# Second layer of a fused attention, MoE and feed-forward kernel: weights requested earlier, into raw buffers alone

## The chip, the cores and the metric

The kernel runs on one core of a Trainium2 chip. TensorE (PE, with PEld for its weight loads) multiplies matrices, VectorE (DVE), ScalarE (ACT) and GpSimd (POOL) do elementwise work, and SyncE (SP) issues most of the DMAs. Each engine executes its own list of instructions strictly in the order in which the program wrote them, and waits at an instruction until the semaphores that it names are reached. What counts is the device time of one execution in microseconds (us).

## The reference

Three stages follow each other. The first is a decayed, unnormalised attention over 8 batches, 8 heads, 576 positions and head size 64. The second is a mixture of 8 experts that sends each of the 4608 tokens (512 numbers each) to one expert. The third, the second layer here, is a dense feed-forward, and the change lies in it:

```python
def _moe2_ref(x, w_in, w_out) -> np.ndarray:      # x: 4608 x 512
    h = x @ w_in                                  # w_in: 512 x 2048
    r = np.maximum(h, 0.0)
    g = r * r
    return (g @ w_out).astype(np.float32)         # w_out: 2048 x 512
```

## The kernel before

**Precision.** Every float32 operand of a large product is split into a rounded part (`hi`) and a remainder (`lo`), and each product is three matmuls, hi by hi, hi by lo and lo by hi. `split` (L1012, L1013) makes the parts: ScalarE writes `hi` with a cast, VectorE then writes `lo` with a subtraction. In the second layer the subtractions are put aside in a list, `los`, and written out where `run_los` is called.

**Tiling of the second layer.** It runs in two passes, one for each half of the 2048 inner columns. A pass goes through nine slots of 512 tokens, and a slot through four quads; so there are 72 quads, numbered 0 to 71, 36 in a pass. Pass one ends with slot 8 (quads 32 to 35), and pass two begins with the same slot (quads 36 to 39). `hquad(n)` multiplies the 512 tokens of the slot by 256 columns of `w_in`. It treats both as 2 by 2 blocks and forms seven products of sums of blocks instead of eight products (Strassen's scheme); that is 42 matmuls of 128x256. Products 1 and 3 go to the PSUM tile `px`, 4 and 2 to `py`, 5 to `pz` (named `pr_all` in the trace), and 7 and 6 are added into `px` again after ScalarE has copied it out. ScalarE copies `px`, `py`, `pz` to the tile `mc`, GpSimd combines them in four operations (L1375 to L1380), VectorE adds the last two products (L1383) and squares what is positive (L1384). The result is split into `gh` (L1387, ScalarE) and `gl` (L1388, VectorE). There is one `mc` tile: the copy of the next quad's `px` waits for `gl` of this quad. `zquad(n)` multiplies `gh` and `gl` by `w_out` (24 matmuls of 128x512) and is written one quad late: TensorE's order is hquad(0), hquad(1), zquad(0), hquad(2), zquad(1), and so on.

**Weights.** The weights of a quad (`WQ`, eight of them, four a pass) are seven sums and plain blocks of `w_in`, split into `wqh` and `wql`. `wq_load` requests the four plain blocks from a scratch tensor `cw`, `wq_sums` forms the five sums on GpSimd (L1041), `wq_split` splits blocks 0 to 3 (128x1024) and then 4 to 6 (128x768). The `w_out` weights of two quads (`WO`, four of them, two a pass) are requested by `wo_load` and split by `wo_split` in two halves. The tokens of a slot are fetched by `x_fetch`, summed by `x_sums` and split by `x_split` and `x_plain` in the same way.

**Buffers.** All these tiles share 20 buffers. `bigt` takes the one that has been idle longest, `drop` gives one back, and the first instruction that writes a taken buffer waits for the last that used it. `wq_load` and `wo_load` take three buffers at once (hi, lo and raw), though only raw, and one block of the hi tile of a `WQ`, are written by the DMAs.

**Order.** It is written out by hand. The table `m2` in `OPT` says at which tick of the last expert slot a step of the second layer stands ('wl 0' is `wq_load(0)`, 'ws' the sums, 'wh' the split). Then comes a branch for rarely needed expert slots (L1329), which no execution here takes. After it, three dictionaries hold the steps of each quad: `before` stands ahead of hquad, `gaps` inside it ahead of the cast to `gh`, `tails` behind zquad of the quad before.

Of the kernel before, what the change touches and what calls it, by code (L numbers as in the profile page):

```python
# [51 lines left out]
def layouts(inputs):  # L52
# [18 lines left out]
    wi = np.ascontiguousarray(inputs["moe2_w_in"].reshape(4, P, 4, 512).transpose(2, 1, 0, 3).reshape(4, P, 2048))  # L71
# [49 lines left out]
    pass  # L121


OPT = dict(manual=True, nbig=10,nlate=10,nx=2,b0=2,bl='SG',rl=2,pz=5,ve=lambda m:'GV' if m<3 or m%4==0 else 'GS',vn=(4,4,2),egn=2,nps=2,npo=1,npt=2,npm=4,nwarm=11,ew=(20,25,32,33),es={23:1,24:1,25:1,26:1,28:1,29:1,30:1,31:1},rlag=1,rlagl=1,rlate=35,rperl=30,e5=5,e6=4,ld=4,rper=8,nw=3,biasat=4,keep=(5,0,4,2),nxw=3,scs=2,e3=13,ylag=2,zlag=2,gb=3,zb=4,cf=(0,6,7,12),cf0=(0,8,9,13),hv=10,zend=1,cwm={0:3},cws={i:(1 if i<4 else 2) for i in range(2,14)},cv0=8,scat=lambda i,n: 2,f3=33,f4=34,f5=34,e0=dict(ro=1,esplit={2:4,3:2,4:2},r1=0,r2=2,r3=2,tab=(7,8,8,9),rec=5,raw=(0,0,1,3),g1=7,split={5:2,6:2,7:2,8:3,9:3,10:2,11:2},xn1=11,tr0=6,tr1=4),hh=3,hl=3,ylag2=1,bs1=dict(regs=1,rec=1,raw=(3,4,5,6),g0=3,g1=7,gn0=(2,)*4,gn1=(2,)*4,split={6:1,7:1,8:2,9:2,10:1,11:2,12:2,13:1,14:2,15:2},tr0=10,tr1=13,cv=1),bs=dict(regs=-9,rec=-9,raw=(0,3,6,8),g0=-4,g1=4,gn0=(1,)*8,gn1=(1,)*8,split={5:1,6:1,7:2,8:2,9:2,10:2,11:2,12:2,13:2},tr0=5,tr1=13,cv=0,f0=7,p0=13,m2={1:('wl 0','xf'),4:('ws 0','xs 0'),5:('xh 0',),6:('wh 0 0',),7:('xs 1',),8:('xh 1',),9:('wh 0 1','wl 1','xs 2'),10:('xh 2','xp 1'),11:('xp 4','ws 1'),12:('wh 1 0',),13:('wh 1 1',)}))


def kernel_body(tc, I, out):
# [1272 lines left out]
    def zquad(n):  # L1400
# [73 lines left out]
    at(gaps, 2, run_los)  # L1474
    for i in range(4):
        at(tails, 32 + i, wq_load, 4 + i)
        at(tails, 33 + i, wq_sums, 4 + i)
        at(gaps, 34 + i, wq_splits, 4 + i)
    for i in range(2):
        at(tails, 34 + 2 * i, wo_load, 2 + i)  # L1480
        at(gaps, 35 + 2 * i, wo_splits, 2 + i)
        at(gaps, 35 + 2 * i, run_los)
    for s in range(len(GSEQ) - 1):
        if s == 8:
            continue
        n, x = 4 * s + (s == 0), s + 1
        at(before, n, x_fetch, x)
        at(tails, n, x_meta, x)
        for i in range(3):
            at(tails, n + i, x_sums, x, i)  # L1490
            d = gaps if n + i + 1 < 4 * x else before
            at(d, n + i + 1, x_split, x, i)
            if i < 2:
                at(gaps, n + i + 1, x_plain, x, (1, 4)[i])
            else:
                at(d, n + i + 1, x_done, x)
# [16 lines left out]
    es.close()

# [14 lines left out]
```

## Time and profile before

| | us |
|---|---|
| median of 3 runs | 1417.16 |
| lowest, highest | 1414.82, 1423.12 |
| the profiled execution | 1433.08 |
| its span, first to last instruction | 1431.3 |
| PE busy in it | 1361.8 (95%) |
| DVE, ACT, POOL busy | 876.4, 517.6, 534.4 |

The profiled execution is a run of its own, taken with the profiler on; all durations of single instructions below come from it. Times of instructions count from the start of its span. The second layer begins at about 634 us and lasts to the end, so it is more than half of the time. Idle time of an engine is given in square brackets ahead of the instruction that ended it, with what it waited for.

### The profile page before, as it was taken

What the parts mean: (1) busy time and instruction counts of PE and PEld (TensorE: products, weight loads), DVE (VectorE), ACT (ScalarE), POOL (GpSimd) and SP (SyncE); (2) the same over time, 40 slices, a digit from 0 to 9 for tenths busy, and PEclk for the clock granted to TensorE, in tenths of its full rate; (3) what the DMA queues carried; (4) which work ended last, traced back from release to release, by engine and by line L of the source; (5) the groups of instructions that cost most, each with busy time, mean ns of one, the idle gap of its engine ahead of it and who ended that gap; (6) DMA issues with size and microseconds to landing.
All of it is one profiled execution on the core that took longest, in us unless ns stands there. A gap on an engine that the chain in (4) does not pass through costs nothing.

```text
span 1431.3 us, 24859 instructions
## 1 busy us (share of the span) xinstructions
PE 1361.8 (95%) x9728; PEld 1191.1 (83%) x9728; DVE 876.4 (61%) x1320; ACT 517.6 (36%) x969; POOL 534.4 (37%) x675
## 2 busy tenths in 40 slices
PE   9999868999999999996999999999989999999996
PEld 7877768988887788896889889898878989989895
DVE  6666747877778677745545454554575556565542
ACT  3223324444344443424433333333443333333321
POOL 0123442644444344224322322223843343434432
PEclk9999979999999999998999999999999999999998
DMA  8788765477655766513111111111231221221210
GB/s 296 215 222 247 204 177 170 139 237 238 208 181 187 243 216 208 164 50 118 59 60 59 31 60 48 43 59 58 91 115 62 89 74 46 88 89 60 88 60 30
DMA packets 105755, 182.08 MB, mean 127 GB/s; under 512 B 25372, under 2 KB 52380, under 8 KB 101276
## 3 DMA queue, kind: packets, MB, share of 16 engines
q1 hardware_dynamic: 96924, 160.96, 36.0%
q0 software_dynamic: 8704, 19.45, 4.4%
q8 instruction: 78, 1.28, 0.4%
q14 instruction: 49, 0.40, 0.1%
HBM read 133.58 MB, written 46.77 MB: 126 GB/s over the span
## 4 chain that ended last, share of the span: by engine, by line
PE 48%; issue 2%; DVE 1%; DMA 1%; ACT 1%; POOL 1%; SPq 0%; POOLq 0%; ACTq 0%; DVEq 0%
PE zp L1420 8%; PE zp L1418 8%; PE zp L1417 8%; PE px L1361 4%; PE px L1363 4%; PE px L1362 4%; PE py L1362 2%; PE py L1363 2%; PE py L1361 2%; PE pr_all L1361 1%; PE pr_all L1363 1%; PE pr_all L1362 1%; DMA wor<-cw 1%; DVE gl L1388 0%; DMA zo<-zA 0%
## 5 line engine op out<-in xcount | busy, mean ns | idle before, releaser
L1417 PE MATMUL zp<-woh,gh 128*128 128x512 f32 x576 | 226.7, 394 | 0.0
L1418 PE MATMUL zp<-wol,gh 128*128 128x512 f32 x576 | 226.6, 393 | 0.0
L1375 POOL TENSOR_TENSOR mc<-mc 128x256 f32<-128x256 f32 x72 | 58.1, 808 | 441.7 <-ACT mc L1374 391.9
L1383 DVE TENSOR_TENSOR mc<-px,mc 128x512 f32<-128x512 f32 x72 | 49.8, 692 | 262.3 <-POOL mc L1379 262.3
L548 POOL DMA_INDIRECT xg<-xl,rix x136 | 139.0, 1022 | 132.5 <-DVE rix L541 75.0
L1420 PE MATMUL zp<-woh,gl 128*128 128x512 f32 x576 | 166.6, 395 | 0.0
L1387 ACT CAST gh<-mc 128x1024 fp32r<-128x1024 f32 x72 | 75.6, 1049 | 237.1 <-DVE mc L1384 233.2
L1388 DVE TENSOR_TENSOR gl<-mc,gh 128x1024 fp32r<-128x1024 f32 x72 | 88.8, 1233 | 90.1 <-ACT gh L1387 90.1
L1420 PEld LDWEIGHTS zp<-woh,gl 128*128 128x128 f32 x576 | 108.5, 188 | 25.2
L1417 PEld LDWEIGHTS zp<-woh,gh 128*128 128x128 f32 x576 | 108.9, 189 | 21.8
L1418 PEld LDWEIGHTS zp<-wol,gh 128*128 128x128 f32 x576 | 108.7, 189 | 21.6
L1361 PE MATMUL px<-xq,wqh 128*128 128x256 f32 x432 | 122.3, 283 | 3.1 <-DVEq L1329 3.1
L639 PE MATMUL yp<-hh,whi 128*128 128x512 f32 (+2 forms) x352 | 123.9, 360 | 1.2 <-ACT hh L619 1.1
L639 PE MATMUL yp<-hh,wlo 128*128 128x512 f32 (+2 forms) x352 | 123.6, 359 | 0.0
L1363 PE MATMUL px<-xq,wql 128*128 128x256 f32 x432 | 122.3, 283 | 1.2 <-DVE wql L1013 1.2
L1362 PE MATMUL px<-xq,wqh 128*128 128x256 f32 x432 | 122.7, 284 | 0.0
L520 DVE TENSOR_TENSOR wlo<-raw,whi 128x512 fp32r<-128x512 f32 x160 | 109.9, 727 | 15.7 <-ACT whi L519 15.1
L1371 ACT COPY mc<-px 128x512 f32<-128x512 f32 x72 | 42.3, 587 | 167.2 <-PE px L1363 143.2
L615 PE MATMUL hp<-xlo,whi 128*128 128x512 f32 (+1 forms) x256 | 98.8, 386 | 0.0
L616 PE MATMUL hp<-xhi,wlo 128*128 128x512 f32 (+1 forms) x256 | 98.7, 385 | 0.0
L614 PE MATMUL hp<-xhi,whi 128*128 128x512 f32 (+1 forms) x256 | 98.7, 385 | 0.0
L519 ACT CAST whi<-raw 128x512 fp32r<-128x512 f32 x160 | 91.0, 618 | 16.2 <-DMA raw<-in_w 14.3
(222 smaller groups left out, 3331.8 us busy)
## 6 DMA issues: line engine op xcount, KB each, us to landing
raw<-in_w SPq DMA_DIRECT2D x34, 1024.0 KB
kqv<-in_kqv SPq DMA_DIRECT2D x108, 256.0 KB
yraw<-yT SPq DMA_DIRECT2D x66, 256.0 KB
zA<-zo SPq DMA_DIRECT2D x36, 256.0 KB
zo<-zA SPq DMA_DIRECT2D x36, 256.0 KB
xl<-xr SPq DMA_DIRECT2D x34, 256.0 KB
craw<-in_wi SPq DMA_DIRECT2D x16, 512.0 KB
cw<-cm SPq DMA_DIRECT2D x32, 256.0 KB
```

The lines of the kernel that those rows point to most:

```text
L520: V.tensor_tensor(out=lo[:, j], in0=raws[i][:, j], in1=hi[:, j].bitcast(F32), op=A.subtract)
L548: G.indirect_dma_start(out=g.x[:, a].rearrange("p k j -> p (k j)"), out_offset=None, in_=xl.rearrange("t (b e) -> (t b) e", b=4)[0:4 * P * ...
L614: PE.matmul(hp, w1h[:, kc, cs], xh[:, kc], start=(kc == 0), stop=False)
L615: PE.matmul(hp, w1h[:, kc, cs], xlo[:, kc], start=False, stop=False)
L616: PE.matmul(hp, w1l[:, kc, cs], xh[:, kc], start=False, stop=(kc == 3))
L639: PE.matmul(hf.yp[dd], w2[:, fb, dd * P:(dd + 1) * P], h, start=start and f == 0 and (w > HW or dd % 2 == 0), stop=stop and f == 7, skip_g ...
L1361: PE.matmul(o, w.hi[:, m, kc], hi[:, kc], start=start and kc == 0, stop=False, skip_group_check=True)
L1362: PE.matmul(o, w.hi[:, m, kc], lo[:, kc], start=False, stop=False, skip_group_check=True)
L1363: PE.matmul(o, w.lo[:, m, kc], hi[:, kc], start=False, stop=stop and kc == 1, skip_group_check=True)
L1417: PE.matmul(zps[s][j], at(gh, j), wh[:, fb], start=(p == 0 and f2 == 0), stop=False)
L1418: PE.matmul(zps[s][j], at(gh, j), wl[:, fb], start=False, stop=False)
L1420: PE.matmul(zps[s][j], at(gl, j), wh[:, fb], start=False, stop=(p == 3 and f2 == 1))
```

## The change

The host lays `w_in` out so that the four plain blocks of a quad stand side by side, in the order in which the raw tile holds them (2, 3, 5, 6; block 6 was 7, and block 5 was kept in the hi tile). A quad's weights are then two DMAs of 128x512 instead of four of 128x2x128. `wq_load` and `wo_load` take the raw buffer alone; the buffers for hi and lo are taken at the first split. The first `w_out` weights are requested and split ahead of the branch: in `m2` the step 'ol 0' (`wo_load(0)`) joins tick 10, and 'oh 0' and 'oh 1' (the two halves of its split) are added as ticks 14 and 15. The steps of quads 0 to 2 and 32 to 37 are placed anew. In every slot the split of plain block 4 of the next slot's tokens moves from the third quad to the fourth.

```diff
     def wq_load(i):
         k = WQ[i] = K()
-        k.hi, k.lo = (bigt(n, F32R, (P, 8, 2, P)) for n in ("wqh", "wql"))
         k.raw = bigt("wqr", F32, (P, 8, 2, P))
-        src = cw[i // 2].rearrange("p (a b) -> p a b", a=4)[:, :, 2 * P * (i % 2):2 * P * (i % 2 + 1)]
-        for t, fb, kh in ((k.raw[:, 2], 0, 0), (k.raw[:, 3], 1, 1), (k.raw[:, 7], 0, 1), (k.hi[:, 7].bitcast(F32), 1, 0)):
-            nc.sync.dma_start(out=t, in_=src[:, 2 * kh:2 * kh + 2, P * fb:P * fb + P])
+        src = cw[i // 2].rearrange("p (q b c d) -> p q b c d", q=2, b=4, c=2)[:, i % 2]
+        for j in range(2):
+            nc.sync.dma_start(out=k.raw[:, 2 + 3 * j:4 + 3 * j], in_=src[:, 2 * j:2 * j + 2])
...
     def wq_split(i, part):
         k, x = WQ[i], slice(4 * part, 4 + 3 * part)
+        if not part:
+            k.hi, k.lo = (bigt(n, F32R, (P, 8, 2, P)) for n in ("wqh", "wql"))
...
     def wo_split(q, h):
-        x = slice(2 * h, 2 * h + 2)
-        split(*(t[:, x] for t in WO[q]))
+        k, x = WO[q], slice(2 * h, 2 * h + 2)
+        if not h:
+            k.hi, k.lo = bigt("woh", F32R), bigt("wol", F32R)
+        split(k.hi[:, x], k.lo[:, x], k.raw[:, x])
...
     at(before, 0, wq_load, 2)
-    at(before, 0, wo_load, 0)
+    at(before, 0, x_fetch, 1)
     at(before, 0, wq_load, 3)
-    at(gaps, 0, wo_splits, 0)
+    at(before, 0, wo_load, 1)
     at(tails, 0, wq_sums, 2)
     at(gaps, 1, wq_splits, 2)
     at(tails, 1, wq_sums, 3)
-    at(tails, 1, wo_load, 1)
     at(gaps, 2, wq_splits, 3)
-    at(gaps, 2, wo_splits, 1)
     at(gaps, 2, run_los)
+    at(posts, 2, wo_splits, 1)
+    at(before, 32, wq_load, 4)
+    at(before, 32, wq_load, 5)
+    at(before, 32, wo_load, 2)
+    at(before, 33, wq_load, 6)
+    at(before, 34, wq_load, 7)
+    at(before, 35, wo_load, 3)
     for i in range(4):
-        at(tails, 32 + i, wq_load, 4 + i)
-        at(tails, 33 + i, wq_sums, 4 + i)
-        at(gaps, 34 + i, wq_splits, 4 + i)
-    for i in range(2):
-        at(tails, 34 + 2 * i, wo_load, 2 + i)
-        at(gaps, 35 + 2 * i, wo_splits, 2 + i)
-        at(gaps, 35 + 2 * i, run_los)
+        at(tails, 32 + i, wq_sums, 4 + i)
+        at(gaps, 33 + i, wq_splits, 4 + i)
+    for h in range(2):
+        at(gaps, 35 + h, wo_split, 2, h)
+        at(gaps, 37, wo_split, 3, h)
+    at(gaps, 37, run_los)
```

The new dictionary `posts` stands behind `gl` of its quad. Where this puts the instructions is seen at three places. TensorE's list is the same in both kernels.

On SP, the first DMAs behind the branch, before the change:

```order
L1034 DMA wqr<-cw 128x2x128 x3
L1034 DMA wqh<-cw 128x2x128
L1053 DMA wor<-cw 128x1024 x2
L1034 DMA wqr<-cw 128x2x128 x3
L1034 DMA wqh<-cw 128x2x128
L1070 DMA yraw<-yT 128x2x256 x4
L1053 DMA wor<-cw 128x1024 x2
```

And with the change (`yraw` are the tokens of the next slot, `wor` the raw `w_out`, `mt` a small table of the slot):

```order
L1034 DMA wqr<-cw 128x512 x2
L1074 DMA yraw<-yT 128x2x256 x4
L1034 DMA wqr<-cw 128x512 x2
L1055 DMA wor<-cw 128x1024 x2
L1080 DMA mt<-meta 128x2x2 x2
```

The first pair of `wor` has moved ahead of the branch, the tokens of slot 1 have moved up in front of the weights of quad 3, and the `wor` left here belongs to quads 2 and 3.

On ScalarE, quads 0 and 1, before the change:

```order
L1371 COPY mc<-px 128x512
L1374 COPY mc<-py 128x2x256
L1378 COPY mc_9649<-pr_all 128x256
L1012 CAST woh<-wor 128x1024 x2
L1387 CAST gh<-mc 128x1024
L1371 COPY mc<-px 128x512
```

With the change:

```order
L1375 COPY mc<-px 128x512
L1378 COPY mc<-py 128x2x256
L1382 COPY mc_9649<-pr_all 128x256
L1391 CAST gh<-mc 128x1024
L1375 COPY mc<-px 128x512
```

The two casts of `w_out` no longer stand between the copies of quad 0 and its cast to `gh`.

On ScalarE, quads 35 to 37, from quad 35's copy of `pz`, before the change:

```order
L1378 COPY mc_13029<-pr_all 128x256
L1012 CAST wqh<-wqr 128x1024
L1012 CAST wqh<-wqr 128x768
L1012 CAST woh<-wor 128x1024 x2
L1387 CAST gh<-mc 128x1024
L1371 COPY mc<-px 128x512
L1374 COPY mc<-py 128x2x256
L1378 COPY mc_13137<-pr_all 128x256
L1012 CAST wqh<-wqr 128x1024
L1012 CAST wqh<-wqr 128x768
L1387 CAST gh<-mc 128x1024
```

With the change:

```order
L1382 COPY mc_13026<-pr_all 128x256
L1013 CAST wqh<-wqr 128x1024
L1013 CAST wqh<-wqr 128x768
L1013 CAST woh<-wor 128x1024
L1391 CAST gh<-mc 128x1024
L1375 COPY mc<-px 128x512
L1378 COPY mc<-py 128x2x256
L1382 COPY mc_13129<-pr_all 128x256
L1013 CAST wqh<-wqr 128x1024
L1013 CAST wqh<-wqr 128x768
L1013 CAST woh<-wor 128x1024
L1391 CAST gh<-mc 128x1024
```

The casts stand at nearly the same places, one half of `w_out` later; the `wqh` here are the weights of one quad further on, and the DMAs that feed all of them are requested two to three quads earlier.

## Rows read from the trace of the kernel before

**Rows 1.** The page's busy line, each engine's time, share and instructions.

```profile
PE 1361.8 (95%) x9728; PEld 1191.1 (83%) x9728; DVE 876.4 (61%) x1320; ACT 517.6 (36%) x969; POOL 534.4 (37%) x675
```

**Rows 2.** Windows: start:end and length, busy time (instructions) by engine, clock, DMA share.

```profile
core 0: us, PE busy (x) PEld busy (x) DVE busy (x) ACT busy (x) POOL busy (x), PEclk, DMA share, GB/s
663.67:675.62 11.95, 10.78 (x68) 9.57 (x66) 8.34 (x9) 5.91 (x9) 5.03 (x6) 1.00 0.00 1
675.62:686.53 10.91, 10.79 (x67) 9.57 (x66) 8.68 (x11) 5.32 (x10) 4.51 (x4) 1.00 0.32 98
686.53:699.16 12.63, 11.12 (x67) 9.63 (x66) 7.20 (x9) 4.56 (x8) 2.90 (x4) 1.00 0.00 0
699.16:1025.70 326.54, 326.54 (x2047) 294.48 (x2046) 164.43 (x204) 117.73 (x192) 104.87 (x137) 1.00 0.17 54
1025.70:1039.21 13.51, 10.84 (x67) 9.55 (x66) 8.33 (x7) 7.44 (x11) 10.98 (x11) 1.00 0.39 121
1049.75:1066.59 16.84, 12.33 (x68) 10.97 (x67) 12.18 (x14) 8.77 (x13) 3.93 (x4) 0.90 0.23 81
1032.10:1035.60 3.50, 3.50 (x21) 3.14 (x22) 0.52 (x1) 2.39 (x4) 2.78 (x4) 1.00 0.87 260
1057.96:1061.40 3.44, 3.44 (x14) 3.31 (x15) 3.44 (x5) 1.38 (x4) 2.71 (x3) 0.52 0.02 5
```

**Rows 3.** Timeline of PE, quads 1 and 2: start, length, instruction, [idle before].

```profile
654.89 0.58 PE L1361 MATMUL px<-xm,wqh 128*128 128x256 f32 x1 [10.24 <-ACT mc L1371]
665.24 0.39 PE L1363 MATMUL px<-xq,wql 128*128 128x256 f32 x1 [1.17 <-DVE wql L1013]
```

**Rows 4.** Timeline of ACT, quads 0 and 1.

```profile
649.31 1.04 ACT L1012 CAST woh<-wor 128x1024 fp32r<-128x1024 f32 x1 [9.18 <-DMA wor<-cw]
650.92 1.05 ACT L1012 CAST woh<-wor 128x1024 fp32r<-128x1024 f32 x1 [0.56 <-DMA wor<-cw]
654.26 0.59 ACT L1371 COPY mc<-px 128x512 f32<-128x512 f32 x1 [1.35 <-DVE gl L1388]
```

**Rows 5.** Timeline of SP, the DMAs it issues, starts of both passes.

```profile
642.80 1.43 SPq L1034 DMA_DIRECT2D wqr<-cw  x3
644.87 0.88 SPq L1053 DMA_DIRECT2D wor<-cw  x2
...
1020.85 0.89 SPq L1053 DMA_DIRECT2D wor<-cw  x2
```

**Rows 6.** Waits of SP from 1010 to 1070 us: total, times, longest.

```profile
SPq L1034 <- DVE wql L1013: 18.3, 1, 18.3
```

**Rows 7.** Timeline of ACT, quad 32 and quads 35 and 37.

```profile
986.63 0.59 ACT L1374 COPY mc<-py 128x512 f32<-128x512 f32 x1 [0.84 <-PE py L1363]
...
1025.45 2.25 ACT L1012 CAST woh<-wor 128x1024 fp32r<-128x1024 f32 x2 [4.47 <-DMA wor<-cw]
...
1050.90 1.05 ACT L1012 CAST woh<-wor 128x1024 fp32r<-128x1024 f32 x1 [5.87 <-DMA wor<-cw]
```

**Rows 8.** Timeline of DVE, quads 0, 1, 31 and 32.

```profile
642.84 1.23 DVE L1384 SCALAR_TENSOR_TENSOR mc<-mc 128x1024 f32<-128x1024 f32 x1
658.69 0.69 DVE L1383 TENSOR_TENSOR mc<-px,mc 128x512 f32<-128x512 f32 x1 [2.25 <-POOL mc L1379]
...
983.52 0.69 DVE L1013 TENSOR_TENSOR xq<-xsum,xq 128x512 fp32r<-128x512 f32 x1
...
992.94 1.23 DVE L1388 TENSOR_TENSOR gl<-mc,gh 128x1024 fp32r<-128x1024 f32 x1 [1.17 <-ACT gh L1387]
```

**Rows 9.** Timeline of POOL, sums for quads 2 and 3.

```profile
645.79 0.72 POOL L1041 TENSOR_TENSOR wqr<-wqr 128x256 f32<-128x256 f32 x1 [3.09 <-DMA wqr<-cw]
...
659.99 1.72 POOL L1041 TENSOR_TENSOR wqr<-wqh,wqr 128x256 f32<-128x256 f32 x1
```

**Rows 10.** Timelines of ACT and DVE, the last ticks ahead of the branch.

```profile
627.17 0.49 ACT L619 ACTIVATE hh<-hp 128x384 fp32r<-128x384 f32 x1 [2.96 <-PE hp L616]
...
630.23 0.56 DVE L652 COPY yo<-yp 128x384 f32<-128x384 f32 x1 [1.99 <-PE yp L639]
```

More of the change, by code (lines that the diff above doesn't have):

```diff
@@ L70, in layouts @@
     o["w2"] = np.ascontiguousarray(inputs["moe_w2"].reshape(E, 2, 4, P, 512).transpose(0, 1, 3, 2, 4).reshape(E, 2, P, 2048))
-    wi = np.ascontiguousarray(inputs["moe2_w_in"].reshape(4, P, 4, 512).transpose(2, 1, 0, 3).reshape(4, P, 2048))
+    wi = inputs["moe2_w_in"].reshape(2, 2, P, 4, 2, 2, P).transpose(3, 2, 4, 5, 0, 1, 6)
+    wi = np.ascontiguousarray(np.stack([wi[:, :, :, f, k] for f, k in ((0, 0), (1, 1), (1, 0), (0, 1))], 3).reshape(4, P, 2048))
     wo = np.ascontiguousarray(inputs["moe2_w_out"].reshape(4, 4, P, 512).transpose(0, 2, 1, 3).reshape(4, P, 2048))
@@ L1029, in wq_load @@
         k = WQ[i] = K()
-        k.hi, k.lo = (bigt(n, F32R, (P, 8, 2, P)) for n in ("wqh", "wql"))
         k.raw = bigt("wqr", F32, (P, 8, 2, P))
-        src = cw[i // 2].rearrange("p (a b) -> p a b", a=4)[:, :, 2 * P * (i % 2):2 * P * (i % 2 + 1)]
-        for t, fb, kh in ((k.raw[:, 2], 0, 0), (k.raw[:, 3], 1, 1), (k.raw[:, 7], 0, 1), (k.hi[:, 7].bitcast(F32), 1, 0)):
-            nc.sync.dma_start(out=t, in_=src[:, 2 * kh:2 * kh + 2, P * fb:P * fb + P])
+        src = cw[i // 2].rearrange("p (q b c d) -> p q b c d", q=2, b=4, c=2)[:, i % 2]
+        for j in range(2):
+            nc.sync.dma_start(out=k.raw[:, 2 + 3 * j:4 + 3 * j], in_=src[:, 2 * j:2 * j + 2])
     def wq_sums(i):
         r = WQ[i].raw
-        a11, a22, a12, a21 = r[:, 2], r[:, 3], r[:, 7], WQ[i].hi[:, 7].bitcast(F32)
-        for n, u, v, op in ((0, a11, a22, A.add), (1, a21, a22, A.add), (4, a11, a12, A.add), (5, a21, a11, A.subtract), (6, a12, a22, A.subtract)):
-            G.tensor_tensor(out=r[:, n], in0=u, in1=v, op=op)
+        for n, u, v, op in ((0, 2, 3, A.add), (1, 5, 3, A.add), (4, 2, 6, A.add), (5, 5, 2, A.subtract), (6, 6, 3, A.subtract)):
+            G.tensor_tensor(out=r[:, n], in0=r[:, u], in1=r[:, v], op=op)
     def wq_split(i, part):
         k, x = WQ[i], slice(4 * part, 4 + 3 * part)
+        if not part:
+            k.hi, k.lo = (bigt(n, F32R, (P, 8, 2, P)) for n in ("wqh", "wql"))
         split(k.hi[:, x], k.lo[:, x], k.raw[:, x])
@@ L1049, in wo_load @@
     def wo_load(q):
-        WO[q] = hi, lo, raw = bigt("woh", F32R), bigt("wol", F32R), bigt("wor")
+        k = WO[q] = K()
+        k.raw = bigt("wor")
         for h in range(2):
             x = slice(2 * h, 2 * h + 2)
-            nc.sync.dma_start(out=raw[:, x], in_=cw[4 + q].rearrange("p (a b) -> p a b", a=4)[:, x])
+            nc.sync.dma_start(out=k.raw[:, x], in_=cw[4 + q].rearrange("p (a b) -> p a b", a=4)[:, x])
     def wo_split(q, h):
-        x = slice(2 * h, 2 * h + 2)
-        split(*(t[:, x] for t in WO[q]))
+        k, x = WO[q], slice(2 * h, 2 * h + 2)
+        if not h:
+            k.hi, k.lo = bigt("woh", F32R), bigt("wol", F32R)
+        split(k.hi[:, x], k.lo[:, x], k.raw[:, x])
         if h:
-            drop_later(WO[q][2])
+            drop_later(k.raw)
     def x_fetch(n):
@@ L1124, in x_last @@
             x_done(0)
-    M2 = dict(wl=wq_load, ws=wq_sums, wh=wq_split, xf=x_first, xs=lambda i: x_sums(0, i), xh=lambda i: x_split(0, i), xp=x_last)
+    M2 = dict(ol=wo_load, oh=lambda h: wo_split(0, h), wl=wq_load, ws=wq_sums, wh=wq_split, xf=x_first, xs=lambda i: x_sums(0, i), xh=lambda i: x_split(0, i), xp=x_last)
     def slot_rec(s):
@@ L1346, in kernel_body, with hquad @@
     SLOT = ((0, 2), (3, 1))
-    def hquad(n, gap):
+    def hquad(n, gap, post):
         s, p = n // 4, n % 4
@@ L1388, in hquad @@
         V.tensor_tensor(out=gl, in0=c, in1=gh.bitcast(F32), op=A.subtract)
+        for fn in post:
+            fn()
         run_los()
@@ L1407, in zquad @@
         gh, gl = gs.pop(n)
-        wh, wl = WO[2 * ph + p // 2][:2]
+        wo = WO[2 * ph + p // 2]
+        wh, wl = wo.hi, wo.lo
         end = n == nq - 1
@@ L1450, in kernel_body @@
     nq = 4 * len(GSEQ)
-    before, gaps, tails = ({} for _ in range(3))
+    before, gaps, posts, tails = ({} for _ in range(4))
     def at(d, n, fn, *a):
@@ L1485, in kernel_body @@
             continue
-        n, x = 4 * s + (s == 0), s + 1
-        at(before, n, x_fetch, x)
+        n, x = 4 * s, s + 1
+        if s:
+            at(before, n, x_fetch, x)
         at(tails, n, x_meta, x)
@@ L1490, in kernel_body @@
             at(tails, n + i, x_sums, x, i)
[L1491 to L1496, printed above, removed]
+            at(gaps, n + i + 1, x_split, x, i)
+        at(gaps, n + 1, x_plain, x, 1)
+        at(gaps, n + 3, x_plain, x, 4)
+        at(gaps, n + 3, x_done, x)
         at(tails, n + 1, x_index, x)
@@ L1504, in kernel_body @@
         run_los()
-        hquad(n, gaps.pop(n, ()))
+        hquad(n, gaps.pop(n, ()), posts.pop(n, ()))
         if n:
@@ L1510, in kernel_body @@
     zquad(nq - 1)
-    assert not before and not gaps and not tails
+    assert not before and not gaps and not posts and not tails
     esC.close()
```

2 lines of the change are left out of this document (1 added, 1 removed).

## The prediction

> **What bounds the kernel now.** I read the busy line first. It names TensorE: PE is busy 95% of the span, and no other engine more than 61% [rows 1]. So no edit that only shortens work of another engine can be worth much, and the question is where PE stands still or runs slowly. The windows by quad answer that. Quads 5 to 35 take 326.54 us with as much PE busy, which is 10.53 us a quad without a gap and at full clock [rows 2]. There the second layer can gain nothing without fewer matmuls. What lies above 10.53 sits in two places, and those are the places that the change touches: the start of pass one and the turn from pass one to pass two.
>
> The start, from PE's timeline: the second product of quad 1 begins at 654.89 after 10.24 us of idle time, which ScalarE's copy of `px` ended, and in quad 2 PE waits again, 1.17 us, for `wql` [rows 3]. The windows that follow add 10.91 and 12.63 for quads 3 and 4, together 2.48 above two steady quads; the tokens of slot 1 are late there [rows 2].
>
> The turn, from the windows: quad 36 takes 13.51 with 10.84 of PE busy, so 2.67 is idle; quad 38 takes 16.84 with 12.33 busy, so 4.51 is idle, and the other 1.80 above a steady quad is slow work: the stretch after that wait ran at a granted clock of 0.52, which is the 1.2 GHz level against 2.4, while the one after the shorter wait of quad 36 kept 1.00 [rows 2]. The excess of the turn is 2.98 + 6.31 = 9.29.
>
> Why PE waits is read backwards from the copy. `mc` is one tile, so the copy of `px` stands behind `gl` of the quad before, and `gl` behind the cast `gh`. At the start ScalarE stood 9.18 and 0.56 us in front of the two casts of `woh`, which stand ahead of `gh` of quad 0, waiting for DMAs that SP could issue only at 644.87, behind the branch; the copy came at 654.26 [rows 4, 5]. At the turn the same cast waits 4.47 and then 5.87 us [rows 7]. Its DMA was issued only at 1020.85, because SP stood 18.3 us at a weight request for the last use of a hi or lo buffer [rows 5, 6].
>
> **The change, part by part.**
>
> *Start, the wait of quad 1.* With both `woh` casts ahead of the branch, the gap of quad 0 is empty. VectorE's squaring starts at 642.84 and takes 1.23, so it ends at 644.07; `gh` ends and `gl` starts 1.17 later (the gap that ScalarE's cast leaves on VectorE in a steady quad), `gl` takes 1.23 [rows 8]: 646.47. The copy of `px` (0.59) then ends at 647.1 instead of 654.85, and PE restarts 7.7 us earlier. Some 2.5 of the 10.24 stay, because one `mc` is still all there is.
>
> *Start, what is late next.* From 654.89 PE worked 9.18 us until it stopped for `wql` at 664.07 (665.24 less 1.17). It did so after 10.24 us of rest; if this cost it what the half clock cost in the stretch of 3.44 us at 0.52, 1.65 us [rows 2, 3], the same work takes 7.5 from 647.1, and PE comes to `wql` of quad 2 at 654.6. That is earlier than the weights. GpSimd starts their sums at 645.79, when their DMA has landed [rows 9], which I take over. Five sums and three combinations for quad 1 stand in its list up to the one that VectorE needs, eight by 0.72 = 5.8, and some will meet VectorE's work and stretch as one of before did, 1.72 against 0.72 [rows 9]; I allow 1.2 for that: 652.8. Before, that product of quad 1 on VectorE started at 658.69 and the matmul on `wql` at 665.24, 6.55 later [rows 3, 8], with the same instructions between. So PE goes on at 659.35, a gain of 5.9. It has then rested 4.7 us, about as long as the 4.51 after which the clock fell, so I charge one such stretch, 3.44 us at 0.52, that is 1.7.
>
> The bounds of this piece: without the stretch and the fall of the clock it gains 7.6; if no sum delayed it at all, 7.7 + 1.17 + 1.65 = 10.5 with the clock kept. If the sums of tokens that now stand ahead on VectorE wait for their DMA (1.5 MB must land from the branch on, and SP needs 1.43 for three requests of the old form [rows 5]), they are late by up to 4, leaving 5.9 − 4 = 1.9. I take the middle value, since each of its durations has a row.
>
> GpSimd and VectorE beside each other deserve a look from the other side. One sum took 1.72 instead of 0.72 with VectorE busy [rows 9]. The Trainium skill, page "SBUF — State Buffer", section "SBUF: two separate sides", calls the port pair that the two share an exclusive lock: a VectorE instruction with two SBUF inputs and a GpSimd instruction that reads SBUF do not run together, and the loser waits for the whole of the other. That speaks against packing the sums beside `gl` and the token sums. By it GpSimd would be held for one `gl` and two token sums, an estimate of 2.6 in place of my 1.2, and the kernel would end 1.4 later than I forecast; the row of 1.72 fits the rule, and it is well inside my range.
>
> *Start, quads 3 and 4.* The tokens of slot 1 are requested a quad earlier, so their waits go: 2.48. Start in all: 5.9 − 1.7 + 2.5 = 6.7.
>
> *Turn.* `wor` for quads 36 and 37, and the weights of quads 36 and 37, are requested in quad 32, those for 38 and 39 in quads 33 to 35, into raw buffers alone. SP then waits only for buffers that earlier splits free, the last at about 1018, and the DMAs land some 15 us ahead of their casts. `woh` of quad 35 no longer waits; the 4.47 and 5.87 us on ScalarE go, and with them the 2.67, the 4.51 and the 1.80 on PE: 9.3. Next late would be the copy for quad 37, by my addition of the listed instructions about 1 us ahead of its need. If this cover is gone it costs what it exceeds.
>
> *Edits at nothing.* Ahead of the branch two casts (1.04, 1.05 [rows 4]) join ScalarE, which has 2.96 idle before `hh`, and two subtractions of about 1.2 (as `gl`, the same size) join VectorE, with 1.99 idle before `yo` [rows 8, 10]. The cover is thin on VectorE; beyond it lies at most 1 us of delay of the expert stage. Two DMAs of longer rows replace four: SP's time, off the path. Splitting plain block 4 a quad later moves one subtraction of 0.69 by some 10 us. In slot 8's case it would follow the one at 983.52 and end near 984.9, and product 5, which needs it, comes after 986.63 [rows 7, 8]: 1.7 to spare.
>
> *Sum.* 6.7 + 9.3 = 16.0. The profiled execution took 1433.08 (span 1431.3 and 1.8 around it); it becomes 1417.1. It lies 15.9 above the median, and as the second layer's waits do not depend on where that surplus is, I subtract the same 16.0 from 1417.16: **1401.2**.
>
> **The rivals.**
>
> *The start goes as well as it can.* Sums early, clock kept: the quads 0 to 4 keep only the 2.5 us of the single `mc`. For it: VectorE's instructions alone would be done early. Against: GpSimd's eight operations do not begin before the DMA. Start 10.5 + 2.5 = 13.0, all 22.3: 1394.9.
>
> *The wait moves to the tokens.* `yraw` for slot 1 now stands in SP's list ahead of the second pair of weights, and VectorE's two sums of it stand ahead of quad 1's last products. If it lands 4 us later than the weights need, the start gives 1.9 − 1.7 + 2.5 = 2.7, all 12.0: 1405.2. For it: 1.5 MB in one place, while SP stood idle with smaller pieces before. Against: SP's queue is otherwise empty there.
>
> *The turn does not deliver.* Raw buffers, too, come from the common 20, and the one idle longest may be one that is not idle; SP then waits as it does now. Only the start remains, 6.7: 1410.5. Against: in steady quads nothing of the weights is split, so raw buffers should lie free.
>
> *The change doesn't do what it says.* Both: 1417.
>
> *Slower.* The later split of plain block 4 is in every slot, 16 times, and in the steady quads any lateness of PE is lost for good, as none idles there. It decides if VectorE runs more than 1.7 us later than at 983.52 in such a quad. At 1.0 us a slot beyond this the 16.0 are eaten, at 1.45 the kernel is 0.5% slower, at 2 it ends at 1433. Against: VectorE was busy 164.43 of 326.54 there [rows 2], so it catches up within a quad.
>
> **How the numbers follow.** The forecast has a chance of 0.60, the better start 0.11, the token wait 0.14, the turn that fails 0.06, no effect 0.04, the slower side 0.05. About 0.5% (7 us) is what a measurement of this kernel can tell from no change, so faster means below 1410.1: the first three whole, and a third of the fourth, 0.87. Same takes no effect, most of the failed turn, and a little of the slower side: 0.09. Slower keeps 0.04. The forecast's own range is 1397 to 1405.5, from the two bounds of the sums and the clock. To leave out no more than 2 in 10 the range reaches to the better start and to the end of the token wait: 1393 to 1408.5.
>
> **What would show it.** Right: PE's wait in quad 1 for the copy falls from 10.24 to about 2.5; a wait of 4 to 5 us for `wql` of quad 2 with a low clock after it; none for `wor` on ScalarE; quads 36 and 38 at about 10.5; steady quads still 10.53. Wrong: a wait on `yraw` at VectorE or SP's request standing in quads 32 to 35; PE waits for `xq` in the fourth quad of slots; an expert stage that ends later than 634. The whole forecast fails if PE's steady quad is no longer 10.53.

## The result and the profile after

The changed kernel takes 1403.01 us (median of 4 runs, 1400.87 to 1408.72), beside 1420.14 for the kernel before in the same session; the ratio of the two is 0.9883, with a 95% interval of 0.9857 to 0.9909. In a second session it was 1397.56 (median of 6 runs) beside 1415.96, ratio 0.9865 (0.9841 to 0.9889). The forecast was 1401.2, a saving of 16.0; the saving measured is 17.1 and 18.4, uncertain by some 3.5 us on either side.

The profiled execution took 1404.08. That is 29.0 less than the profiled execution of before, and 14.2 of it are not the change's. The second layer begins at 620.10 in it and at 634.30 before, and in the sessions below that starting point moves with the session and not with the edits: 616 to 621 where the kernel before took 1416, 629 to 637 where it took 1432 or 1434. So I compare the second layer alone, from PE's first product in it to the end of the span: 1431.3 − 634.30 = 797.0 before, 1402.3 − 620.10 = 782.2 after, 14.8 less. The second profile of the same kernel, from the later session, has 1395.5 − 616.06 = 779.4, so 17.6 less. The forecast of 16.0 lies between the two. Of the kernel before there is only the one profile, so how far its 797.0 would vary is not known.

The busy line after, beside [rows 1]:

```profile
PE 1353.4 (97%) x9728; PEld 1186.9 (85%) x9728; DVE 875.8 (62%) x1320; ACT 517.7 (37%) x969; POOL 531.8 (38%) x675
```

The windows of the quads 2, 3, 4, of the 31 after them, and of quads 36 and 38, beside [rows 2], then 3.46 us behind PE's last wait:

```profile
640.89:657.87 16.98, 12.83 (x67) 11.60 (x66) 12.11 (x15) 7.58 (x11) 8.00 (x8) 0.80 0.00 0
657.87:668.44 10.57, 10.57 (x67) 9.49 (x66) 7.04 (x9) 4.42 (x7) 3.85 (x4) 1.00 0.01 2
668.44:679.00 10.56, 10.56 (x67) 9.48 (x66) 5.30 (x7) 3.68 (x6) 2.90 (x4) 1.00 0.32 99
679.00:1005.80 326.80, 326.80 (x2047) 294.34 (x2046) 166.61 (x205) 120.90 (x195) 112.39 (x143) 1.00 0.18 59
1005.80:1016.35 10.55, 10.55 (x68) 9.48 (x66) 7.01 (x7) 5.74 (x9) 6.35 (x6) 1.00 0.32 101
1026.86:1037.37 10.51, 10.51 (x68) 9.49 (x66) 7.60 (x11) 3.83 (x6) 3.58 (x4) 1.00 0.12 41
645.44:648.90 3.46, 3.46 (x16) 3.46 (x17) 3.46 (x5) 0.59 (x1) 0.53 (x1) 0.50 0.00 0
```

Quads 3 and 4 have lost their 2.4, quad 36 its 2.96 and quad 38 its 6.33: PE has nothing idle there now. The steady quads stand at 326.80 as at 326.54. Quads 0 and 1, which took 663.67 − 634.30 = 29.37, take 640.89 − 620.10 = 20.79. Only quad 2 is longer, 16.98 instead of 11.95. PE's timeline shows why; these are all of its waits from the branch to the end, beside [rows 3]:

```profile
620.10 0.58 PE L1365 MATMUL px<-xq,wqh 128*128 128x256 f32 x1 [3.03 <-DVEq L1333]
633.82 0.39 PE L1365 MATMUL px<-xm,wqh 128*128 128x256 f32 x1 [2.22 <-ACT mc L1375]
645.44 0.58 PE L1367 MATMUL px<-xq,wql 128*128 128x256 f32 x1 [4.15 <-DVE wql L1014]
```

The 10.24 for the copy of `px` have become 2.22, and in quad 2 PE waits 4.15 for `wql`, at half clock behind it (0.50 in the last window, the 1.2 GHz level).

### The profile page after: what moved, and what is told of

Its sections match the earlier page's. It is cut to its first block, busy times and chain, and to the rows that moved or that the text cites. A ratio compares the mean times of both kernels' runs of the same rounds, so it can differ in the third digit from the quotient of the medians.

```text
span 1402.3 us, 24844 instructions
## 1 busy us (share of the span) xinstructions
PE 1353.4 (97%) x9728; PEld 1186.9 (85%) x9728; DVE 875.8 (62%) x1320; ACT 517.7 (37%) x969; POOL 531.8 (38%) x675
## 4 chain that ended last, share of the span: by engine, by line
PE 52%; issue 1%; POOL 1%; DMA 0%; DVE 0%; ACT 0%; POOLq 0%; SPq 0%; DVEq 0%
PE zp L1427 9%; PE zp L1425 9%; PE zp L1424 9%; PE px L1367 5%; PE px L1365 5%; PE px L1366 5%; PE py L1365 2%; PE py L1367 2%; PE py L1366 2%; PE pr_all L1365 1%; PE pr_all L1367 1%; PE pr_all L1366 1%; DMA wqr<-cw 0%; POOL wqr L1040 0%; POOL out L1441 0%
```

## The experiments

Each run is the changed kernel with the edit shown, unless the text says otherwise; times beside it are from its own session, in which the kernel before took the second number. Two readings are needed for the expectations. PE runs hquad(2) behind zquad(0), and what the expectations call quad 1 (16.98) and quad 2 (13.18, 10.57) are quads 2 and 3 of the windows above; "quads 0 and 1" at 37.8 are quads 0 to 2. And second layers of 763 to 776 are counted to the start of the last matmul row, some 12 less than to the end of the span, as I give them; only the 776.5 and the 779 to 782 of the run "The weights split first" are to the end.

**The first w_out weights behind the branch again** (1425.38, before 1434.22).

```diff
-m2={... 10:('xh 2','xp 1','ol 0'), ... 14:('oh 0',),15:('oh 1',)}
+m2={... 10:('xh 2','xp 1'), ...}
     at(before, 0, wq_load, 2)
+    at(before, 0, wo_load, 0)
     at(before, 0, x_fetch, 1)
...
+    at(gaps, 0, wo_splits, 0)
     at(tails, 0, wq_sums, 2)
```

> The changed kernel with one part undone: the first w_out weights are requested and cast behind the branch again, in the gap of quad 0. Theory (the casts of woh ahead of gh set the copy of px of quad 1): PE waits some 10 us for that copy instead of 2.2, the wait of 4.15 for wql of quad 2 shrinks to about 1, quads 0 and 1 together take 41.3 us instead of 37.8, the second layer 785.8 instead of 782.2, the time is some 1406.6. Rival (the start gained because the weights land sooner, in fewer DMAs): PE's wait stays near 2 and the second layer near 782.

PE's waits, then ScalarE's first cast in the gap of quad 0:

```profile
658.49 0.58 PE L1365 MATMUL px<-xm,wqh 128*128 128x256 f32 x1 [11.21 <-ACT mc L1375]
669.50 0.38 PE L1367 MATMUL px<-xq,wql 128*128 128x256 f32 x1 [1.86 <-DVE wql L1014]
```

```profile
653.18 1.04 ACT L1013 CAST woh<-wor 128x1024 fp32r<-128x1024 f32 x1 [10.41 <-DMA wor<-cw]
```

Both waits are back at the sizes expected, and quads 0 to 4 take 64.0, as long as before (64.9) against 56.2 to 58.9 in the eight profiles with the changed start. The second layer is 1425.0 − 636.96 = 788.0, 6 to 9 more than with the change. So the request and the casts behind the branch made the wait, although the new layout and its fewer DMAs stayed.

**The turn's steps at their old places, raw buffers alone** (1426.32, before 1434.22).

```diff
-    at(before, 32, wq_load, 4)
...
-    at(before, 35, wo_load, 3)
     for i in range(4):
-        at(tails, 32 + i, wq_sums, 4 + i)
-        at(gaps, 33 + i, wq_splits, 4 + i)
-    for h in range(2):
-        at(gaps, 35 + h, wo_split, 2, h)
-        at(gaps, 37, wo_split, 3, h)
-    at(gaps, 37, run_los)
+        at(tails, 32 + i, wq_load, 4 + i)
+        at(tails, 33 + i, wq_sums, 4 + i)
+        at(gaps, 34 + i, wq_splits, 4 + i)
+    for i in range(2):
+        at(tails, 34 + 2 * i, wo_load, 2 + i)
+        at(gaps, 35 + 2 * i, wo_splits, 2 + i)
+        at(gaps, 35 + 2 * i, run_los)
```

> The changed kernel with the steps of quads 32 to 37 at their places of before, but still raw buffers alone. Theory (SP was held by the three buffers taken at once): SP is not held, ScalarE does not wait for wor, quads 36 and 38 stay at 10.5, the second layer at 782. Rival (the requests had to be written earlier): quads 36 and 38 go back to about 13.5 and 16.8, the second layer to 791.5, the time to some 1412.

```profile
1023.23 0.39 PE L1365 MATMUL px<-xm,wqh 128*128 128x256 f32 x1 [2.60 <-ACT mc L1375]
1048.50 0.39 PE L1365 MATMUL px<-xm,wqh 128*128 128x256 f32 x1 [3.87 <-ACT mc L1375]
```

```profile
990.46 1.15 SPq L1055 DMA_DIRECT2D wor<-cw  x2
...
1036.12 1.10 SPq L1055 DMA_DIRECT2D wor<-cw  x2
```

```profile
1012.04 2.00 ACT L1013 CAST woh<-wor 128x1024 fp32r<-128x1024 f32 x2
...
1041.59 1.05 ACT L1013 CAST woh<-wor 128x1024 fp32r<-128x1024 f32 x1 [5.43 <-DMA wor<-cw]
```

My theory fell here. SP is no longer held, `wor` is requested at 990.46 and ScalarE casts it in quad 35 without a wait, and still PE waits 2.60 in quad 36 and 3.87 in quad 38: 13.43 and 16.20 us, nearly as before. The raw buffers alone gave the turn next to nothing.

**As that, and three buffers taken at once for pass two** (1426.58, before 1434.22).

```diff
     def wq_load(i):
         k = WQ[i] = K()
+        if i > 3:
+            k.hi, k.lo = (bigt(n, F32R, (P, 8, 2, P)) for n in ("wqh", "wql"))
...
     def wo_load(q):
         k = WO[q] = K()
+        if q > 1:
+            k.hi, k.lo = bigt("woh", F32R), bigt("wol", F32R)
```

> As the run with the old places, and hi, lo and raw buffers of the weights of pass two taken at once again (the start stays as changed). Theory: SP is held some 18 us again, quads 36 and 38 take 13.5 and 16.8, the second layer 791.5, the time is some 1412. Rival (the layout of w_in or the transfers gave the gain of the turn): quads 36 and 38 stay near 10.5, the second layer near 782.

```profile
1023.30 0.58 PE L1369 MATMUL px<-xm,wqh 128*128 128x256 f32 x1 [2.88 <-ACT mc L1379]
1048.38 0.39 PE L1369 MATMUL px<-xm,wqh 128*128 128x256 f32 x1 [2.21 <-ACT mc L1379]
```

```profile
SPq L1036 <- DVE wql L1014: 17.0, 1, 17.0
```

SP is held 17.0 again, and quads 36 and 38 take 15.19 and 13.00, together 28.2, no more than in the run without the hold (29.6); the ratios to the kernel before are 0.9958 and 0.9955. So at the old places SP's wait of 18.3 [rows 6] was real and cost nothing of its own: something else was as late. Two more runs name it, one for each quad.

**One request moved back: wo_load(3)** (1418.33, before 1431.84).

```diff
-    at(before, 35, wo_load, 3)
+    at(tails, 36, wo_load, 3)
```

> The changed kernel with one request moved back: wo_load(3), the w_out weights of quads 38 and 39, behind zquad(35) as before, so behind the four stores of zA on SP. Theory from the run with old places (there SP issued it at 1036.12, after stores that wait for zo, and ScalarE waited 5.43 us): quad 38 alone goes back to about 16.2 us, quad 36 stays at 10.5; the second layer is 5.7 longer than that of the changed kernel, some 776. Rival (quad 38 was late because of the subtractions on VectorE): quad 38 stays near 10.5.

```profile
1047.67 0.39 PE L1365 MATMUL px<-xm,wqh 128*128 128x256 f32 x1 [3.54 <-ACT mc L1375]
```

```profile
1030.01 5.78 SPq L1436 DMA_DIRECT2D zA<-zo  x4
1035.88 1.00 SPq L1055 DMA_DIRECT2D wor<-cw  x2
```

```profile
1040.73 1.05 ACT L1013 CAST woh<-wor 128x1024 fp32r<-128x1024 f32 x1 [6.70 <-DMA wor<-cw]
```

Quad 38 alone takes 15.89; quad 36 stays at 10.54. The request stands on SP behind four stores of `zA`, which go out from 1030.01 to 1035.79.

**The subtractions ahead of gl** (1417.14, before 1431.84).

```diff
-    for h in range(2):
-        at(gaps, 35 + h, wo_split, 2, h)
-        at(gaps, 37, wo_split, 3, h)
-    at(gaps, 37, run_los)
+    for i in range(2):
+        at(gaps, 35 + 2 * i, wo_splits, 2 + i)
+        at(gaps, 35 + 2 * i, run_los)
```

> The changed kernel, requests as early as in it, but both halves of the w_out split in the gap of quad 35 (and of 37) and the pending subtractions written out there, ahead of gl, as before. Theory (in the run with old places wor had landed, and gl of quad 35 stood behind four subtractions of 6.6 us): PE waits 2.6 us for the copy of px in quad 36, that quad takes 13.4; quad 38 stays near 10.5 to 11; the second layer is some 3 longer than that of the changed kernel, 773. Rival (a late DMA makes the wait of quad 36): quad 36 stays at 10.5.

```profile
1019.63 0.39 PE L1365 MATMUL px<-xm,wqh 128*128 128x256 f32 x1 [2.61 <-ACT mc L1375]
```

VectorE in quad 35, and ScalarE's casts there:

```profile
1011.24 3.18 DVE L1014 TENSOR_TENSOR wql<-wqr,wqh 128x1024 fp32r<-128x1024 f32 x2
1014.34 3.43 DVE L1014 TENSOR_TENSOR wol<-wor,woh 128x1024 fp32r<-128x1024 f32 x2
1017.69 1.21 DVE L1392 TENSOR_TENSOR gl<-mc,gh 128x1024 fp32r<-128x1024 f32 x1
```

```profile
1008.45 2.00 ACT L1013 CAST woh<-wor 128x1024 fp32r<-128x1024 f32 x2
1011.40 1.05 ACT L1391 CAST gh<-mc 128x1024 fp32r<-128x1024 f32 x1 [0.95 <-DVE mc L1388]
1018.99 0.58 ACT L1375 COPY mc<-px 128x512 f32<-128x512 f32 x1 [6.54 <-DVE gl L1392]
```

Quad 36 alone takes 13.42, quad 38 10.51. No DMA is late; `gl` stands behind 6.6 us of subtractions although `gh` was ready at 1012.45.

**The old layout of w_in** (1412.39, before 1431.84).

```diff
-        for j in range(2):
-            nc.sync.dma_start(out=k.raw[:, 2 + 3 * j:4 + 3 * j], in_=src[:, 2 * j:2 * j + 2])
+        for t, fb, kh in ((2, 0, 0), (3, 1, 1), (6, 0, 1), (5, 1, 0)):
+            nc.sync.dma_start(out=k.raw[:, t], in_=src[:, 2 * kh:2 * kh + 2, P * fb:P * fb + P])
```

> The changed kernel with w_in in the layout of before and four DMAs of 128x2x128 for the weights of a quad, into the raw tile. Theory (the layout is off the path): the second layer stays within 0.7 us of 770.1, except that the sums of quad 2 may start up to 0.7 later, as they did at 11.49 instead of 10.77 after the start of the layer. Rival (the gain at the start is due to fewer DMAs): quad 1 takes 2 us more, 772 or above.

The second layer is 1416.2 − 635.64 = 780.6, between the two profiles of the changed kernel, and the ratio of the times is 0.9873 (0.9853 to 0.9893). In the expectation's count it is 768.5, outside the 0.7 that I allowed around 770.1, but on the side away from the rival's 772: quad 2 took 14.64, with a wait of 2.46 for `wql`. The layout is worth nothing that these runs can tell.

**Plain block 4 in the third quad again** (1400.41, before 1415.96).

```diff
-        at(gaps, n + 3, x_plain, x, 4)
+        at(gaps, n + (3 if s in (0, 9) else 2), x_plain, x, 4)
```

> The changed kernel with plain block 4 split in the third quad of the slot again, as before, except in the first slot of each pass. Theory: steady quads have VectorE to spare, so they stay at 10.53 and 31 of them at 326.8, the second layer within 0.5 us of the changed kernel's. Rival (the later split costs in every slot): the 31 quads take some 7 us less.

The window of the 31 steady quads:

```profile
678.87:1005.67 326.80, 326.80 (x2048) 294.33 (x2047) 166.53 (x204) 120.88 (x195) 112.42 (x143) 1.00 0.18 59
```

326.80 with either place; the edit costs nothing in steady quads. (The change moves this split in 15 slots; in the first slot the place was the same before.) The second layer is 780.8, between the two profiles of the changed kernel.

**The tokens of slot 1 a quad later** (1405.18, before 1415.96).

```diff
-    at(before, 0, x_fetch, 1)
...
-        n, x = 4 * s, s + 1
-        if s:
-            at(before, n, x_fetch, x)
+        n, x = 4 * s + (s == 0), s + 1
+        at(before, n, x_fetch, x)
...
-            at(gaps, n + i + 1, x_split, x, i)
+            d = gaps if n + i + 1 < 4 * x else before
+            at(d, n + i + 1, x_split, x, i)
```

> The changed kernel with the tokens of slot 1 requested, summed and split a quad later, as before. Theory (the waits of quads 3 and 4 before were for these tokens): quads 3 and 4 take 10.9 and 12.6 instead of 10.57 and 10.56, the second layer is 2.4 longer; the wait for wql of quad 2 may shrink, as two token sums stand no more in front of it on VectorE. Rival (those waits came from the late weights of quads 2 and 3): quads 3 and 4 stay at 10.6.

```profile
669.61 0.39 PE L1366 MATMUL py<-xq,wqh 128*128 128x256 f32 x1 [1.13 <-DVE xq L1014]
671.98 0.58 PE L1365 MATMUL pr_all<-xq,wqh 128*128 128x256 f32 x1 [0.79 <-ACT xq L1013]
```

```profile
671.98:675.40 3.42, 3.19 (x13) 2.90 (x14) 0.76 (x2) 1.29 (x3) 2.08 (x3) 0.50 0.00 0
```

Quad 4 takes 16.35 instead of 10.56: its waits add up to 2.15 (1.51 idle before [rows 2]), and here the clock fell to half behind them. Quad 3 stays at 10.54, so its 0.38 of before was not the tokens'. The second layer is 786.8, 4.6 to 7.3 more. The wait for `wql` shrinks to 1.78, with quads 0 to 2 together at 35.9, no better than the 35.1 to 37.8 with the tokens early.

**The weights split first** (1417.12, before 1434.22).

```diff
+        for fn in mid:
+            fn()
         V.tensor_tensor(out=c[:, 0:2], in0=px, in1=c[:, 0:2], op=A.add)
...
-    at(gaps, 1, wq_splits, 2)
+    at(mids, 1, wq_splits, 2)
+    at(mids, 1, run_los)
...
-    at(gaps, 2, wq_splits, 3)
-    at(gaps, 2, run_los)
+    at(mids, 2, wq_splits, 3)
+    at(mids, 2, run_los)
```

`mids` is a new dictionary, whose steps stand ahead of the last addition on VectorE.

> The changed kernel with the weights of quads 2 and 3 split ahead of the last addition on VectorE (mc<-px,mc) of quads 1 and 2, instead of behind their gl. Theory (what is late at quad 2 is only the order on VectorE, as wqh is cast 9 us before): the wait of 4.15 for wql and the half clock behind it go, quad 1 takes about 10.6 to 11.5 instead of 16.98, the second layer about 776.5, the time is some 1397. Rival (the addition held up there delays gl, and PE then waits for the copy of px of quad 2): a wait of 2 to 4 us at that copy, second layer 779 to 782.

```profile
672.39 0.39 PE L1365 MATMUL px<-xm,wqh 128*128 128x256 f32 x1 [2.34 <-ACT mc L1375]
```

```profile
669.87 1.99 ACT L1013 CAST woh<-wor 128x1024 fp32r<-128x1024 f32 x2
671.76 0.57 ACT L1375 COPY mc<-px 128x512 f32<-128x512 f32 x1
```

Quad 2 falls to 10.63, and quad 3 waits in its place, 13.18 (the copy of `px` behind two casts of `woh`). Quads 0 to 4 take 56.25, against 58.1 and 58.0 in the two runs of the session with the changed start. The second layer is 779.5, as the rival had it.

**Spread over more quads** (1413.86, before 1431.84).

```diff
-    at(posts, 2, wo_splits, 1)
+    at(gaps, 2, wo_splits, 1)
+    at(posts, 2, run_los)
...
+                at(tails, n + i + (i == 1 and not s), x_sums, x, i)
+                at(gaps, n + i + 1 + (i == 1 and not s), x_split, x, i)
...
+            at(posts, 3, run_los)
+            at(posts, 3, x_sums, 1, 2)
+            at(before, 4, x_split, 1, 2)
```

> The kernel that splits first, with the casts of the second w_out weights moved ahead of gh of quad 2, and the second and third token sums of slot 1 a quad later, so that VectorE is less crowded in quad 2. Theory (the wait of 2.34 for the copy of px of quad 3 came from the two casts of woh in front of it and from VectorE's full list in quad 2): that wait goes, quad 2 takes 10.6 instead of 13.18, the second layer about 764.9. Rival (slot 1's last token sums are now late for quad 4): a wait for xq in quad 3 or 4, second layer 766 to 769.

```profile
669.94 0.38 PE L1365 MATMUL px<-xm,wqh 128*128 128x256 f32 x1 [0.15 <-ACT mc L1375]
679.49 0.39 PE L1366 MATMUL py<-xq,wqh 128*128 128x256 f32 x1 [0.80 <-DVE xq L1014]
```

The copy's wait falls to 0.15, and quad 4 waits for tokens, as the rival had it: 12.54. Quads 0 to 4: 55.7.

**The same, with quad 0's combinations on VectorE** (1398.36, before 1415.96; the changed kernel beside it 1397.56).

```diff
-        G.tensor_tensor(out=c[:, 1], in0=c[:, 1], in1=c[:, 3], op=A.subtract)
+        E_ = G if n else V
+        E_.tensor_tensor(out=c[:, 1], in0=c[:, 1], in1=c[:, 3], op=A.subtract)
...
+                at(mids if i == 1 and not s else gaps, n + i + 1 + (i == 1 and not s), x_split, x, i)
...
+            at(mids, 3, run_los)
+            at(mids, 3, x_sums, 1, 2)
+            at(gaps, 3, x_split, 1, 2)
```

> The spread kernel with two more edits: VectorE, which idles there, forms the four combinations of quad 0 in GpSimd's place, and the second token sums of slot 1 are split in quad 3 ahead of the last addition on VectorE. Theory: the four combinations took 0.7 us each in a row on GpSimd, so the copy of px of quad 1 comes 1 to 1.5 earlier and its wait falls from 2.6 to 1.2 or so; quad 4 loses its waits of 0.80 and 0.67 and takes 10.6; the second layer is about 763.3, the time some 5 to 6 us less than that of the changed kernel. Rival (VectorE is slower at these, or quad 4 waits for another operand): 766 or more.

```profile
642.20 0.58 PE L1365 MATMUL px<-xm,wqh 128*128 128x256 f32 x1 [2.82 <-ACT mc L1375]
```

PE's first wait falls to 1.65, and the next one moves to the copy in quad 2: 14.87, with the clock at 0.58 behind it. Quad 4 keeps a wait of 0.67 for `xq` and takes 11.49. The four combinations were done 1.4 earlier, and then VectorE waited 3.6 for the tokens' DMA. Quads 0 to 4 take 55.97, the kernel beside it 56.2. The expected 5 to 6 us did not come.

**The changed kernel once more**, beside the last three.

> The changed kernel once more, beside the others of this chip. Theory (the waits come from the order on the engines): the same three waits of PE in the second layer and no other, some 2.5 for the copy of quad 1 and 2.4 to 4.9 for wql of quad 2, second layer 768.5 to 771; against the kernel before 16 to 17 us less. Rival (part of the first difference lay ahead of the second layer, by chance): some 15 us less.

```profile
640.72 0.39 PE L1367 MATMUL px<-xq,wql 128*128 128x256 f32 x1 [3.48 <-DVE wql L1014]
```

```profile
640.72:644.20 3.48, 3.48 (x29) 3.48 (x30) 3.48 (x5) 1.14 (x2) 0.54 (x1) 1.00 0.00 0
```

The same waits, 2.31 and 3.48, but the clock stayed at full behind the second: 779.4 in place of 782.2. The saving is 18.4, more than the 16 to 17 expected, and 17.6 of it lie in the second layer.

## Why the prediction was right, point by point

*Quad 1.* I put PE's restart 7.7 earlier and 2.5 of the wait as staying; it came 6.9 earlier (13.72 us after the layer's start instead of 20.59) with 2.22 of wait. The 0.8 are quad 0, which took 7.78 instead of 6.63, as it ran at 0.50 for its first 6.0 us behind the branch, less 0.3 of wait. The run with the casts behind the branch shows the mechanism. One reading was wrong: the product that waits is not the second of quad 1 but product 7, the sixth written; its operand is `xm`. The chain behind the wait is the same.

*What is late next.* The chain named was the one that ended last. VectorE and GpSimd in quad 1, VectorE first:

```profile
635.04 2.42 DVE L1096 TENSOR_TENSOR xsum<-yraw 128x512 f32<-128x512 f32 x2 [1.94 <-DMA yraw<-yT]
638.90 0.69 DVE L1387 TENSOR_TENSOR mc<-px,mc 128x512 f32<-128x512 f32 x1 [1.44 <-POOL mc L1383]
...
643.64 3.14 DVE L1014 TENSOR_TENSOR wql<-wqr,wqh 128x1024 fp32r<-128x1024 f32 x2
```

```profile
632.09 3.66 POOL L1040 TENSOR_TENSOR wqr<-wqr 128x256 f32<-128x256 f32 x4 [0.49 <-DMA wqr<-cw]
635.71 1.20 POOL L1379 TENSOR_TENSOR mc<-mc 128x256 f32<-128x256 f32 x1
636.98 1.07 POOL L1380 TENSOR_TENSOR mc<-mc 128x256 f32<-128x256 f32 x1
```

VectorE's addition starts 18.80 after the start of the layer (I had 652.8 − 634.3 = 18.5), and PE goes on 6.54 later (6.55). The gain up to here is 30.94 − 25.34 = 5.6; I had 5.9. (One bound was mis-added: without the 1.2 for stretched sums the gain is 7.1, not 7.6; the forecast does not use it.) The tokens' DMA made VectorE wait 1.94, hidden behind GpSimd's combinations by 1.44: the rival of the tokens missed by that much. GpSimd lost 0.81 in two combinations (1.20 and 1.07 instead of 0.73 each) beside the token sums, which took 1.21 each instead of 0.69: both engines were slowed. The exclusive lock of the Trainium skill, page "SBUF — State Buffer", section "SBUF: two separate sides", would have put the addition at 19.9 by the estimate made from it; 18.80 is nearer to my value. By the rows both engines lost, where the rule lets one of them wait.

*The clock.* I charged 1.7 because the wait would be as long as the 4.51 before. The stretch behind it ran at 0.50, and PE was busy 12.83 in that quad instead of 10.78, so it cost 2.05; in the second profile, behind 3.48, it ran at 1.00 and cost nothing. That the charge came near in the first profile is luck: the length of the wait alone does not decide it (below). The start, forecast at 6.7, gave 5.6 − 2.05 + 2.41 = 6.0 in the first profile and 8.7 in the second.

*Quads 3 and 4.* 2.48 forecast, 2.41 measured. With the tokens late again quad 4 alone takes 5.8 more, since the clock falls behind its waits, and quad 3 nothing. So the sum was near, but not all of it was the tokens'. What gave quad 3 its 0.38 was not tried.

*The turn.* 9.3 forecast, 2.96 + 6.33 = 9.3 measured, and here the reasons were half wrong. I read quad 36's wait as one for `wor`, whose DMA SP issued late because of three buffers taken at once. The rows were right; but without that DMA's wait the same 2.6 remain, because the subtractions stood ahead of `gl`. VectorE's row of quad 35 in the trace of before could have told it:

```profile
1026.54 3.17 DVE L1013 TENSOR_TENSOR wol<-wor,woh 128x1024 fp32r<-128x1024 f32 x2 [0.20 <-ACT woh L1012]
```

ScalarE had waited 4.47 for the DMA, but VectorE, busy with other subtractions, stood only 0.20 for the cast behind it. `gl` began at 1029.63, though `gh` had ended at 1028.65. So two causes lay beside each other, the subtractions the later by about 1 us, and the change removed both; that it also moves the subtractions of quad 35 behind `gl` has no price in my prediction, and that its number holds for quad 36 is luck. In quad 38 the wait was for `wor`, as I had it (15.89 in the run with that request moved back), but what kept the request back were the stores of `zA` ahead of it in SP's list. The change moved the request in front of them. The step that failed is that the 2.67 of quad 36 goes with ScalarE's 4.47, and that taking three buffers at once is what made the requests late: it is the places of the steps, not the buffers alone, that carry the 9.3 (13.43 and 16.20 us with raw buffers alone, 10.55 and 10.51 with the places too).

Two of my signs of being wrong came and cost nothing: VectorE's wait on `yraw` (1.94, above), and SP's requests, which still stood in quads 33 to 35 (waits of SP from 980 to 1060 us, total, times, longest):

```profile
SPq L1034 <- DVE wql L1014: 10.5, 1, 10.5
SPq L1055 <- DVE wql L1014: 9.7, 1, 9.7
```

Even so `wor` for quads 38 and 39 was requested at 998.84, and ScalarE cast it from 1020.37 on without a wait. What I had put next late, the copy for quad 37 with 1.0 to spare, waited 0.97 for its product and for nothing else:

```profile
1017.97 0.59 ACT L1375 COPY mc<-px 128x512 f32<-128x512 f32 x1 [0.97 <-PE px L1367]
```

What the buffers give is that the new places are possible. This is a count in the kernel and not a run: at quad 32, 16 of the 20 buffers are in use (eight `wqh` and `wql`, four `woh` and `wol`, three `xq`, one `xm`). The three requests written there take three raw buffers; with hi and lo taken at once they would need nine.

*At nothing.* The layout, plain block 4 and the steady quads: shown by the runs, 780.6 and 326.80. The casts ahead of the branch cannot be told from the start of the second layer, which differs by session. But in the trace of the change VectorE, done with the second subtraction, still waits for PE, as ScalarE does (1.18):

```profile
616.06 0.56 DVE L653 COPY yo<-yp 128x384 f32<-128x384 f32 x1 [0.44 <-PE yp L640]
```

The measured saving exceeds that of the second layer by 2.3 in the first session and 0.8 in the second; both are inside the interval, and where they come from stays open.

## What to carry to other kernels

A wait in the trace names what came last, and there may be a second cause of the same size right behind it: before crediting a wait's removal to one edit, ask what would stand ahead of the waiting instruction if that DMA had landed, and read how long the engine next in the chain stood for it (here 0.20 of 4.47). In lists executed in order, the place of a request behind stores that wait, and of remainders ahead of the operand that another engine needs, was worth 5.4 and 2.9 us, while held buffers by themselves, at the old places, cost nothing. Where a start is bound by several engines at once, moving one step hands the wait to the next quad, as three attempts here showed (55.7 to 56.3 us for five quads instead of 56.2 to 58.9, and no gain in time clear of noise).

## What the runs showed of the hardware

PE's clock did not follow the length of the wait. Behind a wait of 3.48 us it stayed at 1.00 and behind 2.67 too [rows 2], while behind waits of 2.43 and 2.46, in the runs with the subtractions ahead and with the old layout, these stretches ran at 0.54, the first window being of the former:

```profile
653.61:657.00 3.39, 3.39 (x16) 3.39 (x17) 3.39 (x5) 0.58 (x1) 0.52 (x1) 0.54 0.00 0
```

```profile
660.02:663.50 3.48, 3.48 (x17) 3.48 (x18) 3.48 (x5) 0.59 (x1) 0.53 (x1) 0.54 0.00 0
```

In the run with the tokens late even a wait of 1.78 had 0.53 behind it. Behind the wait of 2.2 to 2.6 in quad 1 the next 3.4 us ran at 1.00 in three of the eight profiles with the changed start, and at 0.64 to 0.68 in the other five. So the same start, in one of the eight with the old DMAs of `w_in`, took 56.2 to 58.9 us for quads 0 to 4. What decides it was not tried.
